# A backward kernel's gelu derivative as three two-step operations instead of five single ones

## The chip, the core and the metric

One core of a Trainium2 chip. The time is the device time of one execution in microseconds; below it is the median of three runs. The core has a matmul engine (TensorE, PE; its weight loads are listed apart as PEld), VectorE (DVE), ScalarE (ACT), GpSimd (POOL) and SyncE (SP), each with its own instruction queue worked in order, and 16 DMA engines.

## What is computed

The forward function is a small speech joint network; the kernel returns its output and the gradients of all seven inputs. Everything is bfloat16.

```python
B, T, D, K, U = 2, 16000, 256, 3, 8
def _fwd_reference(x, w1, w2, g, w_f, w_g, w_o):
    h = conv(x, w1)                    # 3 taps, padded, D -> D
    h = _gelu(h)[:, ::2, :]            # tanh form of gelu, every second row
    f = conv(h, w2)
    f = _gelu(f)[:, ::2, :]
    fe = jnp.einsum("btd,de->bte", f, w_f)
    ge = jnp.einsum("bud,de->bue", g, w_g)
    j = jnp.tanh(fe[:, :, None, :] + ge[:, None, :, :])
    return jnp.einsum("btud,dv->btuv", j, w_o)

out, vjp = jax.vjp(f, x, w1, w2, g, w_f, w_g, w_o)
return (out, *vjp(grad_out))           # grad_out: [2, 4000, 8, 256]
```

(`conv` stands for the reference's pad and loop over the three taps.) The tanh form of gelu is x times sigmoid(A (x + 0.044715 x^3)) with A = 2 sqrt(2/pi). With s the sigmoid, its derivative is s + x s (1 - s) A (1 + 3 * 0.044715 x^2).

## The kernel before

The 4,000 joint positions of each of the two batches lie on one axis of 8,016 columns, with a gap of 16 between them. It is cut into 16 chunks of 512 columns (`CW`), the last of 336. Channels lie on the partitions, in two halves (`KT`), so an activation of one chunk is a tile of 128 partitions by 2 x 512.

A chunk goes through these stages, each written as a generator that yields after a piece of work:

- `conv_units`: the first convolution, on even and odd positions (`par` 0 and 1), then a gelu on each: `HT` is the activation, `G1` the derivative.
- `conv2_units`: the second convolution and its gelu: `FT` and `G2`.
- `fe_units`, then for each of the 8 prompts `u` a `tanh` (ACT, L423).
- `joint_units`: the output matmuls (L721), the gradient of `w_o` (`gwo`, L760), and `gj`: matmuls of `grad_out` with the transposed `w_o` into PSUM (L672), which DVE evicts as `NGZ` times the tanh's derivative (L676). The square that this needs, `JSQ`, is ACT's (L664). POOL adds up the eight NGZ (L695) in `ACCN`; the last sum is `NGFE`.
- backward, of the chunk before: `d1_units` (NGFE times transposed `w_f`, evicted by DVE as `GF` with the factor `G2`, L462), `d5_units` (GF times transposed `w2`, evicted as `GH` with the factor `G1`, L486), `row_units`, `gwf_units`, `gw2_units`, `ghr_units` and `e_units` (transposes, weight gradients, the gradient of x; L496, L546, L564, L627, L640).

The main loop (L865) runs over the chunks n = 0 to 15; one pass is called a step here and takes about 49.8 us when steady. In step n, `weave` alternates the joint's units of chunk n with a fill: the convolutions of chunk n + 1 and the backward stages of chunk n - 1. The work of a gelu does not stand in these generators. `gelu` (L287) returns two lists of operations. `first` (square, sum, sigmoid, product) makes the activation and goes into the queue `later`, which `weave` pumps two at a time. `second` makes the derivative. Those of a chunk's three gelus go into the queue `late` when its second convolution is through (L381), that of the second convolution first, then `seconds0`, those of the two parities; behind them stands a one-column copy of `G1` from the chunk before, on POOL (L352). `late` is pumped one at a time and emptied at the end of the step (L904). From chunk 2 on its operations are pinned, that is, kept in program order with each other; elsewhere the compiler's scheduler may reorder instructions that don't depend on each other.

In `gelu`, `x_` is the convolution's value, `sq_` the square 0.044715 x^2, `s_` first the sum and then the sigmoid, `h_` the activation and `gp_` the derivative.

Matmul results go through a PSUM pool of 7 tiles (`psp`, L124), which are given out in turn, whatever the stage; the eighth, `GWO_ps`, is kept for the gradient of `w_o`. Scratch tiles of a gelu have three buffers each (`gel`), NGZ three (`ngzp`), JSQ two (`jsp`), the rows of the x gradient two (`gxp`).

Of the kernel before, what the change touches and what calls it, by code (L numbers as in the profile page):

```python
# [15 lines left out]
ALU = mybir.AluOpType  # L16
# [2 lines left out]
GELU_K = 0.044715  # L19
GELU_R = float(np.sqrt(0.044715))  # L20
GELU_A = float(2.0 * np.sqrt(2.0 / np.pi))

P = 128
KT = 2
# [4 lines left out]
CW = 512  # L29
# [3 lines left out]
def kernel(  # L33
# [22 lines left out]
    nc = tc.nc  # L56
# [7 lines left out]
    def geom(n):  # L64
        c0 = n * CW
        return c0, min(CW, L - c0)
# [60 lines left out]
    def ps_f32():  # L127
        return psp.tile([P, 512], FP32, name="ps", tag="ps")
# [22 lines left out]
    S = [dict() for _ in range(G)]  # L151
# [111 lines left out]
    def scratch(name, spare):  # L263
        if spare:
            return rowp.tile([P, 8, P], BF16, name="rows")[:].rearrange("p (k a) b -> p k (a b)", k=KT)
        return gel.tile([P, KT, CW], BF16, name=name)
# [17 lines left out]
    def pinned(op, n):  # L284
        return op if n <= 1 else (lambda: tc.keep_in_program_order(op()))

    def gelu(xb, W, h, gp, off, kts=((0, KT),), spare=False):  # L287

        sq, s = scratch("g_sq", spare), scratch("g_s", spare)
        TT, TS, STT = nc.vector.tensor_tensor, nc.vector.tensor_scalar, nc.vector.scalar_tensor_tensor  # L290
        first, second = [], []
        for (k0, k1) in kts:
            sq_, s_, x_ = sq[:, k0:k1, :W], s[:, k0:k1, :W], xb[:, k0:k1, :W]
            h_, gp_ = h[:, k0:k1, off:off + W], gp[:, k0:k1, off:off + W]
            first += [
                partial(nc.scalar.activation, out=sq_, in_=x_, func=ACT.Square, scale=GELU_R),
                partial(STT, out=s_, in0=sq_, scalar=1.0, in1=x_, op0=ALU.add, op1=ALU.mult),
                partial(nc.scalar.activation, out=s_, in_=s_, func=ACT.Sigmoid, scale=GELU_A),
                partial(TT, out=h_, in0=s_, in1=x_, op=ALU.mult),
            ]  # L300
            second += [
                partial(TS, out=sq_, in0=sq_, scalar1=3.0 * GELU_A, scalar2=GELU_A, op0=ALU.mult, op1=ALU.add),
                partial(TS, out=x_, in0=s_, scalar1=-1.0, scalar2=1.0, op0=ALU.mult, op1=ALU.add),
                partial(TT, out=sq_, in0=sq_, in1=x_, op=ALU.mult),
                partial(TT, out=sq_, in0=sq_, in1=h_, op=ALU.mult),
                partial(TT, out=gp_, in0=sq_, in1=s_, op=ALU.add),
            ]
        return first, second


    HALVES = ((0, 1), (1, 2))

    seconds0 = []

    def conv_units(n):
        c0, W = geom(n)
        seconds = []
        st = S[n]
        HT = htp.tile([P, 2, KT, CW + 2], BF16, name="HT")
        G1 = g1p.tile([P, 2, KT, CW + 2], BF16, name="G1")  # L320
        st["HT"], st["G1"] = HT, G1
        if n == G - 1:
            nc.gpsimd.memset(G1[:, 0, :, 2 + W:3 + W], 0.0)
        if n == 0:
            nc.gpsimd.memset(HT[:, 1, :, 1:2], 0.0)
            nc.gpsimd.memset(G1[:, 1, :, 1:2], 0.0)
        else:
            nc.gpsimd.tensor_copy(out=HT[:, 1, :, 1:2], in_=S[n - 1]["HT"][:, 1, :, CW + 1:CW + 2])
        taps = {0: ((1, 0, 0), (2, 1, 0), (0, 3, -1)), 1: ((0, 1, 0), (2, 3, 0), (1, 2, 0))}
        for par in range(2):  # L330
            xb = gel.tile([P, KT, CW], BF16, name="g_x")
            for mt in range(KT):
                ps = ps_f32()
                k = 0
                for (i, c, sh) in taps[par]:
                    for kt in range(KT):
                        nc.tensor.matmul(ps[:, :W], lhsT=W1[:, i, kt, mt * P:(mt + 1) * P],  # L337
                                         rhs=st["X", c][:, kt, 16 + sh:16 + sh + W], start=(k == 0), stop=(k == 5))
                        k += 1
                nc.scalar.copy(out=xb[:, mt, :W], in_=ps[:, :W])  # L340
                yield
            first, second = gelu(xb, W, HT[:, par], G1[:, par], 2, HALVES if n == 0 else ((0, KT),))
            if par == 1 and n > 1:
                for j in (1, 3):
                    first[j] = partial(lambda f: held.append(f()), first[j])
            later.extend(first)
            seconds += second
            if n == 0:
                pump(len(first))
        seconds0.extend(seconds)  # L350
        if n > 0:
            seconds0.append(lambda: nc.gpsimd.tensor_copy(out=G1[:, 1, :, 1:2],  # L352
                                                          in_=S[n - 1]["G1"][:, 1, :, CW + 1:CW + 2]))

    def conv2_units(n):
        c0, W = geom(n)
        st = S[n]
        HT = st["HT"]
        if n > 0:
            pump(len(later))  # L360
        FT = packed(ftp.tile([P, KT, CW], BF16, name="FT")[:], "k w", n, k=KT)
        G2 = ftp.tile([P, KT, CW], BF16, name="G2")
        st["FT"], st["G2"] = FT, G2
        xb = scratch("g_x", n == 0)
        for mt in range(KT):
            ps = ps_f32()
            k = 0
            for (i, par, off) in ((1, 0, 2), (0, 1, 1), (2, 1, 2)):
                for kt in range(KT):
                    nc.tensor.matmul(ps[:, :W], lhsT=W2[:, i, kt, mt * P:(mt + 1) * P],  # L370
                                     rhs=HT[:, par, kt, off:off + W], start=(k == 0), stop=(k == 5))
                    k += 1
            nc.scalar.copy(out=xb[:, mt, :W], in_=ps[:, :W])
            yield
        first, second = gelu(xb, W, FT, G2, 0, HALVES if n == 0 else ((0, KT),), n == 0)
        if n == 0:
            for f in first:
                f()
        else:
            later.extend(first)  # L380
        late.extend(pinned(f, n) for f in second + seconds0)  # L381
        seconds0.clear()
        late_open[0] = True
# [62 lines left out]
    def d1_units(n):  # L446
        c0, W = geom(n)
        st = S[n]
        GF = gfp.tile([P, KT, CW + 4], BF16, name="GF")
        st["GF"] = GF  # L450
        if n > 0:
            nc.gpsimd.tensor_copy(out=GF[:, :, 1:2], in_=S[n - 1]["GF"][:, :, CW + 1:CW + 2])
        else:
            nc.gpsimd.memset(GF[:, :, 1:2], 0.0)
        if n == G - 1:
            nc.gpsimd.memset(GF[:, :, 2 + W:3 + W], 0.0)
        for mt in range(KT):
            ps = ps_f32()
            for kt in range(KT):
                nc.tensor.matmul(ps[:, :W], lhsT=WFT[:, kt, mt * P:(mt + 1) * P], rhs=st["NGFE"][:, kt, :W],  # L460
                                 start=(kt == 0), stop=(kt == KT - 1))
            nc.vector.scalar_tensor_tensor(out=GF[:, mt, 2:2 + W], in0=st["G2"][:, mt, :W], scalar=-1.0,  # L462
                                           in1=ps[:, :W], op0=ALU.mult, op1=ALU.mult)
            yield

    def d5_units(n):
        st = S[n]
        c0, W = geom(n)
        N = W + 1 if n == G - 1 else W
        GF, G1 = st["GF"], st["G1"]  # L470
        GH = ghp.tile([P, 2, KT, CW + 4], BF16, name="GH")
        st["GH"] = GH
        if n == 0:
            nc.gpsimd.memset(GH[:, 0, :, 1:2], 0.0)
        else:
            nc.gpsimd.tensor_copy(out=GH[:, 0, :, 1:2], in_=S[n - 1]["GH"][:, 0, :, CW + 1:CW + 2])
        for par, taps in ((0, ((1, 0),)), (1, ((2, -1), (0, 0)))):
            for mt in range(KT):
                ps = ps_f32()
                k, last = 0, len(taps) * KT - 1  # L480
                for (i, sh) in taps:
                    for kt in range(KT):
                        nc.tensor.matmul(ps[:, :N], lhsT=W2T[:, i, kt, mt * P:(mt + 1) * P],  # L483
                                         rhs=GF[:, kt, 2 + sh:2 + sh + N], start=(k == 0), stop=(k == last))
                        k += 1
                gh = nc.vector.tensor_tensor(out=GH[:, par, mt, 2:2 + N], in0=ps[:, :N],  # L486
                                             in1=G1[:, par, mt, 2 - par:2 - par + N], op=ALU.mult)
                while held:
                    tc.add_manual_dep(held.pop().ins, gh.ins.name, NOSYNC, reason="held")
                yield  # L490
# [421 lines left out]
    n = G - 1  # L912
# [75 lines left out]
```

## Time and profile before

| | us |
|---|---|
| median of 3 runs | 823.95 |
| all three | 828.51, 820.92, 823.95 |
| the profiled execution | 822.13 |
| its span in the profile | 820.4 |

A span is the time from the first to the last instruction that the profile shows; the execution's own time has 1.7 us more around it. The profile gives for every engine its busy time, its instructions and what it waited for. A group "L277 DVE SCALAR_TENSOR_TENSOR g_s<-g_sq,g_x" is line 277 of the kernel, engine, operation, written tile and read tiles. "x29 | 60.8, 2097" is 29 instructions, 60.8 us busy, 2,097 ns mean. Two instructions of one engine can overlap by a little: the next starts when the one before is in its last stretch, so the distance from start to start is shorter than the duration. A number in brackets behind a row of the timeline is idle time of the engine ahead of it and what ended it.

Two things of the profile are used below: the TensorE clock is granted at 0.995 over the span, and the pattern of a step repeats from step 1 to step 13 to within some 10 ns in most steps (the one around 350 to 400 us holds the gap between the batches).

### The profile page before, as it was taken

How to read it: one execution, taken by the hardware profiler on the slowest of the kernel's cores; microseconds unless marked ns; L12 is line 12 of the kernel's file. 1: busy time of each engine (PE TensorE's matmuls, PEld its weight loads, DVE VectorE, ACT ScalarE, POOL GpSimd, SP SyncE). 2: the span in 40 equal slices, each digit the busy share in tenths (PEclk: the TensorE clock that was granted, in tenths of full speed). 3: DMA queues.
4: the chain of work that ended last, by engine and by line, in shares of the span. 5: the costliest groups of instructions: out<-in, count | busy, mean ns of one | idle time of the engine just before them, and what ended most of it. 6: DMA issues, size and time to landing. Idle time of an engine off the chain costs nothing.

```text
span 820.4 us, 16444 instructions
## 1 busy us (share of the span) xinstructions
PE 797.0 (97%) x6234; PEld 593.2 (72%) x6310; DVE 623.8 (76%) x1190; ACT 677.1 (83%) x1076; POOL 394.4 (48%) x419
## 2 busy tenths in 40 slices
PE   8888999999999999999999999999999999999998
PEld 3455777868678676777767778676786777778796
DVE  4995786877869778697887878868697786968634
ACT  4988997896979969799797978969799697988643
POOL 1265553553544535545476634535455345445551
PEclk9999999999999999999999999999999999999999
DMA  9989999999999999999999999999999999999944
GB/s 213 236 187 250 236 258 244 249 235 181 275 257 241 228 211 209 253 245 196 248 234 220 241 196 237 255 250 272 218 249 221 261 231 251 246 226 272 242 121 142
DMA packets 401423, 189.38 MB, mean 231 GB/s; under 512 B 349296, under 2 KB 385048, under 8 KB 401344
## 3 DMA queue, kind: packets, MB, share of 16 engines
q1 hardware_dynamic: 381104, 121.43, 80.5%
q0 software_dynamic: 20240, 66.89, 27.1%
q8 instruction: 49, 0.80, 0.5%
q14 instruction: 30, 0.25, 0.1%
HBM read 51.39 MB, written 50.34 MB: 124 GB/s over the span
## 4 chain that ended last, share of the span: by engine, by line
PE 82%; ACT 8%; DMA 4%; DVE 3%; issue 1%; SPq 1%; POOL 0%; POOLq 0%; DVEq 0%; ACTq 0%
PE GWO_ps L760 12%; PE ps L721 12%; PE ps L672 10%; PE ps L640 9%; PE ps L627 9%; PE ps L337 7%; PE ps L564 5%; PE pst L496 5%; PE ps L370 4%; PE ps L483 4%; ACT JT L423 3%; DMA JR<-JT 3%; PE ps L546 2%; PE ps L460 1%; ACT JSQ L664 1%
## 5 line engine op out<-in xcount | busy, mean ns | idle before, releaser
L695 POOL TENSOR_TENSOR ACCN<-ACCN,NGZ 128x1024 f32<-128x1024 f32 (+1 forms) x80 | 169.3, 2117 | 76.2 <-DVE NGZ L676 75.3
L676 DVE SCALAR_TENSOR_TENSOR NGZ<-JSQ,ps 128x512 bf16<-128x512 bf16 (+3 forms) x272 | 168.4, 640 | 41.0 <-PE ps L672 31.2
L723 ACT CAST OUT<-ps 128x512 bf16<-128x512 f32 (+1 forms) x252 | 145.8, 595 | 38.4 <-PE ps L721 38.3
L423 ACT ACTIVATE JT<-FE,GE 128x512 bf16<-128x512 f32 (+3 forms) x272 | 176.2, 711 | 0.5
L664 ACT ACTIVATE JSQ<-JT 128x1024 bf16<-128x1024 bf16 (+1 forms) x128 | 134.9, 1059 | 36.2 <-DVE NGZ L676 36.1
L721 PE MATMUL ps<-WO,JT 128*128 128x256 bf16 (+1 forms) x1008 | 150.6, 274 | 3.5 <-DVE NGZ L676 3.4
L760 PE MATMUL GWO_ps<-GO,JR 128*128 128x256 bf16 (+1 forms) x1008 | 149.2, 273 | 2.7 <-DMA JR<-JT 1.8
L748 POOL DMA_DIRECT2D out_dram<-OUT x76 | 55.8, 734 | 172.3 <-ACT OUT L723 156.0
L672 PE MATMUL ps<-GOT,WOT 128*128 128x512 bf16 (+1 forms) x481 | 132.6, 374 | 1.4 <-DVE W2T L845 1.0
L760 PEld LDWEIGHTS <-JR 128*128 128x128 bf16 (+1 forms) x1008 | 97.1, 98 | 29.5 <-DMA JR<-JT 3.7
L721 PEld LDWEIGHTS <-JT 128*128 128x128 bf16 (+1 forms) x1008 | 97.9, 99 | 25.8 <-issue 4.6
L627 PE MATMUL ps<-W1T,GH 128*128 128x256 bf16 (+2 forms) x756 | 100.4, 273 | 0.7
L277 DVE SCALAR_TENSOR_TENSOR g_s<-g_sq,g_x 128x1024 bf16<-128x1024 bf16 (+2 forms) x35 | 67.6, 1930 | 36.7 <-ACT g_sq L277 36.7
L627 PEld LDWEIGHTS <-GH 128*128 128x128 bf16 (+2 forms) x756 | 83.5, 116 | 13.0
L337 PE MATMUL ps<-XC,W 128*128 128x512 bf16 (+1 forms) x358 | 85.9, 377 | 1.7 <-DMA XC<-in_x_dram 1.0
L640 PE MATMUL ps<-rows,XR 128*128 128x256 bf16 (+1 forms) x708 | 84.7, 273 | 0.0
L444 DVE TENSOR_TENSOR ACC<-ACC,ps 128x512 f32<-128x512 f32 x84 | 57.5, 684 | 32.6 <-PE ps L564 26.2
L630 ACT CAST GX<-ps 128x512 bf16<-128x512 f32 (+2 forms) x126 | 72.3, 588 | 7.8 <-PE ps L627 5.2
L640 PEld LDWEIGHTS <-XR 128*128 128x128 bf16 (+1 forms) x708 | 69.3, 98 | 11.0
L259 POOL DMA_DIRECT2D out_dram<-GX x66 | 36.2, 549 | 82.8 <-ACT GX L630 81.3
L672 PEld LDWEIGHTS <-WOT 128*128 128x128 bf16 x512 | 48.2, 98 | 33.5 <-issue 2.1
L337 PEld LDWEIGHTS <-W 128*128 128x128 bf16 x384 | 37.7, 99 | 39.7 <-issue 2.1
(132 smaller groups left out, 1218.4 us busy)
## 6 DMA issues: line engine op xcount, KB each, us to landing
GO<-in_grad_out_dram SPq DMA_DIRECT2D x56, 512.0 KB, 5.7
out_dram<-OUT POOLq DMA_DIRECT2D x56, 512.0 KB, 6.0
out_dram<-GX POOLq DMA_DIRECT2D x55, 256.0 KB, 5.0
XR<-in_x_dram POOLq DMA_DIRECT2D x36, 256.0 KB, 7.8
XR<-in_x_dram POOLq DMA_DIRECT2D x12, 320.0 KB, 8.1
GO<-in_grad_out_dram SPq DMA_DIRECT2D x4, 384.0 KB, 4.9
out_dram<-OUT POOLq DMA_DIRECT2D x4, 384.0 KB, 4.4
GOT<-in_grad_out_dram SPq DMA_TRANSPOSE x68, 6.6
```

The source lines that it names most:

```text
L337: nc.tensor.matmul(ps[:, :W], lhsT=W1[:, i, kt, mt * P:(mt + 1) * P], rhs=st["X", c][:, kt, 16 + sh:16 + sh + W], start=(k == 0), stop=(k ...
L423: act = nc.scalar.activation(out=JT[:, mt, lo:hi], in_=S[n]["FE"][:, mt, lo:hi], func=ACT.Tanh, bias=GE[:, b, mt, u:u + 1], scale=1.0)
L627: nc.tensor.matmul(ps[:M, cj * D:(cj + 1) * D], lhsT=GH[:, par, kt, o:o + s * (M - 1) + 1:s], rhs=W1T[:, i, kt, :], start=(j == 0), stop=( ...
L630: nc.scalar.copy(out=t[:M, 2 * cp:2 * cp + 2, :], in_=ps[:M, :])
L640: nc.tensor.matmul(ps[:, dt * D:(dt + 1) * D], lhsT=x_row(4 * k + i + 2 * (1 - par))[:M, dt * P:(dt + 1) * P], rhs=t[:M, g + 2 * par:g + 2 ...
L664: jsq = nc.scalar.activation(out=JSQ[:, :, :W], in_=JT[:, :, :W], func=ACT.Square)
L672: nc.tensor.matmul(ps[:, :W], lhsT=WOT[:, kt, mt * P:(mt + 1) * P], rhs=GOT[:, kt, :W], start=(kt == 0), stop=(kt == KT - 1))
L676: nc.vector.scalar_tensor_tensor(out=NGZ[:, mt, lo:hi], in0=JSQ[:, mt, lo:hi], scalar=1.0, in1=ps[:, lo:hi], op0=ALU.subtract, op1=ALU.mul ...
L695: st["last"] = nc.gpsimd.tensor_tensor(out=out, in0=in0, in1=st["NGZ", u][:, :, :W], op=ALU.add)
L721: nc.tensor.matmul(ps[:M, j * V:(j + 1) * V], lhsT=st["JT", u][:, kt, o:o + M], rhs=WO[:, kt, :], start=(kt == 0), stop=(kt == KT - 1))
L723: nc.scalar.copy(out=OUT[:M, k, :], in_=ps[:M, :])
L760: nc.tensor.matmul(GWO_ps[:, dt, :], lhsT=JR[:M, j, dt, k, :], rhs=GO[:M, k, j * V:(j + 1) * V], start=(n_gwo[0] == 0), stop=(n_gwo[0] == ...
```

## The change

The list `second` of a gelu has five single operations per pair of halves: two on one tensor (`tensor_scalar`), three on two (`tensor_tensor`). For all chunks but the first it becomes three `scalar_tensor_tensor`, each of which does (in0 op0 scalar) op1 in1:

- sq = (sq + 1/3) * x
- sq = (s - 1) * sq
- gp = (sq + 1/SLOPE) * s

with SLOPE = -3 A. The result is the derivative divided by SLOPE. The factor SLOPE is put back where the derivative is used: as the scalar of GF's eviction, which has one already, and of GH's, which turns from `tensor_tensor` into `scalar_tensor_tensor`. Chunk 0 keeps the five operations and the factor 1. The copied column of G1 carries the factor of the chunk before, so POOL's copy becomes a multiplication by the ratio of the factors. The activation `h_` and the overwriting of `x_` are no longer part of the derivative.

```diff
+SLOPE = -3.0 * GELU_A
...
-    def gelu(xb, W, h, gp, off, kts=((0, KT),), spare=False):
+    def gelu(xb, W, h, gp, off, kts=((0, KT),), spare=False, scaled=True):
...
             second += [
+                partial(STT, out=sq_, in0=sq_, scalar=1.0 / 3.0, in1=x_, op0=ALU.add, op1=ALU.mult),
+                partial(STT, out=sq_, in0=s_, scalar=1.0, in1=sq_, op0=ALU.subtract, op1=ALU.mult),
+                partial(STT, out=gp_, in0=sq_, scalar=1.0 / SLOPE, in1=s_, op0=ALU.add, op1=ALU.mult),
+            ] if scaled else [
                 partial(TS, out=sq_, in0=sq_, scalar1=3.0 * GELU_A, scalar2=GELU_A, op0=ALU.mult, op1=ALU.add),
                 partial(TS, out=x_, in0=s_, scalar1=-1.0, scalar2=1.0, op0=ALU.mult, op1=ALU.add),
                 partial(TT, out=sq_, in0=sq_, in1=x_, op=ALU.mult),
                 partial(TT, out=sq_, in0=sq_, in1=h_, op=ALU.mult),
                 partial(TT, out=gp_, in0=sq_, in1=s_, op=ALU.add),
             ]
...
+    def slope(n):
+
+        return SLOPE if n else 1.0
...
-            first, second = gelu(xb, W, HT[:, par], G1[:, par], 2, HALVES if n == 0 else ((0, KT),))
+            first, second = gelu(xb, W, HT[:, par], G1[:, par], 2, HALVES if n == 0 else ((0, KT),), scaled=n > 0)
...
-            seconds0.append(lambda: nc.gpsimd.tensor_copy(out=G1[:, 1, :, 1:2],
-                                                          in_=S[n - 1]["G1"][:, 1, :, CW + 1:CW + 2]))
+            seconds0.append(lambda: nc.gpsimd.tensor_scalar(out=G1[:, 1, :, 1:2], in0=S[n - 1]["G1"][:, 1, :, CW + 1:CW + 2],
+                                                            scalar1=slope(n - 1) / slope(n), scalar2=None, op0=ALU.mult))
...
-        first, second = gelu(xb, W, FT, G2, 0, HALVES if n == 0 else ((0, KT),), n == 0)
+        first, second = gelu(xb, W, FT, G2, 0, HALVES if n == 0 else ((0, KT),), n == 0, n > 0)
...
-            nc.vector.scalar_tensor_tensor(out=GF[:, mt, 2:2 + W], in0=st["G2"][:, mt, :W], scalar=-1.0,
+            nc.vector.scalar_tensor_tensor(out=GF[:, mt, 2:2 + W], in0=st["G2"][:, mt, :W], scalar=-slope(n),
...
-                gh = nc.vector.tensor_tensor(out=GH[:, par, mt, 2:2 + N], in0=ps[:, :N],
-                                             in1=G1[:, par, mt, 2 - par:2 - par + N], op=ALU.mult)
+                gh = nc.vector.scalar_tensor_tensor(out=GH[:, par, mt, 2:2 + N], in0=G1[:, par, mt, 2 - par:2 - par + N],
+                                                    scalar=slope(n), in1=ps[:, :N], op0=ALU.mult, op1=ALU.mult)
```

## The prediction

> **What bounds the kernel now.** I read the page first, then the busy time of one 49.8 us step, then the Vector engine's groups by shape, then the engines' timelines inside that step. Parts 1 and 4 of the page:
>
> ```profile
> PE 797.0 (97%) x6234; PEld 593.2 (72%) x6310; DVE 623.8 (76%) x1190; ACT 677.1 (83%) x1076; POOL 394.4 (48%) x419
> ...
> PE 82%; ACT 8%; DMA 4%; DVE 3%; issue 1%; SPq 1%; POOL 0%; POOLq 0%; DVEq 0%; ACTq 0%
> ```
>
> The matmul engine works 97% of the span and carries 82% of the chain of waits. The busy time of one steady stretch (294.6 to 344.4 us) is tighter still; the columns are busy us of PE, weight loads, DVE, ACT, POOL, then clock and DMA:
>
> ```profile
> 294.60:344.40 49.80, 49.53 (x391) 37.09 (x394) 39.05 (x70) 42.51 (x68) 23.74 (x24) 1.00 1.12 241
> ```
>
> PE is idle 0.27 us of 49.80, and in the list of waits it waits for the Vector engine (DVE) nowhere between 140 and 690 us but for 0.2 us. So DVE has 10.75 us to spare per step and no work of its own on the path. The change touches DVE alone in size; it can gain nothing inside the steady steps, and lose only where DVE becomes so late that PE lacks something. What PE can lack is a PSUM tile: the pool has 7, given out in turn, so a tile is opened again seven openings later.
>
> **What the change puts on DVE.** Durations by shape, in the DVE groups (mean ns of one, idle before):
>
> ```profile
> L285 DVE TENSOR_SCALAR g_sq<-g_sq 128x1024 bf16<-128x1024 bf16 x39 | 16.5, 423 | 0.4
> ...
> L285 DVE TENSOR_TENSOR g_sq<-g_sq,FT 128x1024 bf16<-128x1024 bf16 x13 | 9.0, 691 | 0.4
> ```
>
> A gelu's derivative is now two one-tensor operations (0.42 each) and three two-tensor ones (0.69 each): 2.91 us when nothing disturbs. The new form is three scalar_tensor_tensor of 128x1024 bf16, both inputs in SBUF. That instruction is already in the kernel (g_s, L277). Undisturbed, early in the run:
>
> ```profile
> 31.72 1.21 DVE L277 SCALAR_TENSOR_TENSOR g_s<-g_sq,g_x 128x1024 bf16<-128x1024 bf16 x1
> 32.86 0.67 DVE L676 SCALAR_TENSOR_TENSOR NGZ<-JSQ,ps 128x512 bf16<-128x512 bf16 x1
> ```
>
> 1.21 us, the next independent instruction starting 1.14 after it; where the next one needs its result or overwrites its input it is 1.26 (another g_s starts at 53.20, its follower at 54.46). So three cost 3.63: the change adds 0.72 us per gelu, 2.2 per step, while it drops the instruction count from 15 to 9.
>
> The Trainium skill speaks for the change here: "VectorE: DVE Perf Modes", rules for kernel authors, says of chained Vector operations to keep the number of operations low, since each pays its pipeline drain. By that rule 9 for 15 would shorten DVE's work and the sum below would be zero. These rows disagree: three at 1.21 against five at 2.91.
>
> 2.2 us would vanish in the 10.75 idle if it were spread. It is not. All three derivatives of the next chunk stand together at the end of a step, between the g_s of the second convolution and the last gradient evictions NGZ (L676) of the step. I walk this place in the step at 295 us. The built program's PE order there is unchanged, instruction by instruction; DVE's is new: after g_s come first-F, ACC, FT, second-F, third-F, first-H, ACC, second-H, third-H, first-H', second-H', NGZ a, third-H', NGZ b (F: second convolution, H and H': first). Before, DVE runs so:
>
> ```profile
> 306.50 0.69 DVE L676 SCALAR_TENSOR_TENSOR NGZ<-JSQ,ps 128x512 bf16<-128x512 bf16 x1 [0.41 <-PE ps L672]
> ...
> 307.72 0.68 DVE L676 SCALAR_TENSOR_TENSOR NGZ<-JSQ,ps 128x512 bf16<-128x512 bf16 x1
> ...
> 309.87 1.17 DVE L285 TENSOR_SCALAR g_x<-g_s 128x1024 bf16<-128x1024 bf16 x1
> ...
> 312.27 2.50 DVE L285 TENSOR_TENSOR g_sq<-g_sq,HT 128x1024 bf16<-128x1024 bf16 x1
> ```
>
> NGZ a starts at 306.50, NGZ b at 307.72 and ends at 308.40. In the new order the first new instruction starts where the old one did, at 298.95. Up to NGZ b there are nine new instructions, six followed at 1.14 and three at 1.26 (10.62), two ACC at a pitch of 0.60, FT at 0.61 and NGZ a at 0.61: 13.04, so NGZ b starts at 311.99 and ends at 312.67, 4.27 late. NGZ a ends at 310.92, 3.73 late.
>
> Who waits for that: PE's weight loads show the openings of PSUM tiles (L640 is one tile of 16, L627 one of 6, L672 one of 2, L721 one of 4):
>
> ```profile
> 305.69 0.64 PEld L672 LDWEIGHTS <-WOT 128*128 128x128 bf16 x4
> 306.45 1.84 PEld L640 LDWEIGHTS <-XR 128*128 128x128 bf16 x16
> 308.30 0.21 PEld L672 LDWEIGHTS <-WOT 128*128 128x128 bf16 x2
> 308.63 0.76 PEld L627 LDWEIGHTS <-GH 128*128 128x128 bf16 x6
> 309.39 0.21 PEld L672 LDWEIGHTS <-WOT 128*128 128x128 bf16 x2
> 309.71 0.77 PEld L627 LDWEIGHTS <-GH 128*128 128x128 bf16 x6
> 310.48 0.86 PEld L721 LDWEIGHTS <-JT 128*128 128x128 bf16 x8
> ```
>
> The first row opens two tiles, those of NGZ a and b. Count seven on from b: L640, L672, L627, L672, L627, L721, L721. The second L721 tile, at 310.48 + 0.43 = 310.91, is b's buffer. It has 2.51 us to spare after 308.40; a's buffer (first L721) has 3.29 after 307.19. New: b is free at 312.67, with about 0.05 to start, so PE stands still from 310.91 to 312.72: **1.8 us per step**, the 0.5 that a costs included. PE makes it up nowhere, having 0.27 us of idle. The ACC and NGZ behind b (before at 308.66, 309.26, 310.95) become 4.0, 4.0 and 2.9 late against 2.9, 3.2 and 2.7 of room: inside the 1.8. Then DVE has caught up.
>
> The other edits, each beside this:
> - FT comes about 0.6 us later (300.69 for 300.05); its matmul starts at 302.32, and FT now ends at 301.4. Nothing; without that cover it would be as much per step.
> - GF's scalar: none. GH's eviction turns from tensor_tensor (687 ns at 128x512, L486) into scalar_tensor_tensor with one PSUM input; the same shape at L462 takes 680. Nothing.
> - POOL's column copy (0.2 us, 15 times) becomes tensor_scalar, for which there is no row: between 0.2 and the 2.1 of a full POOL addition; I take 0.2, same shape. It also moves up in POOL's queue, ahead of a GX store and the last two additions (ACCN, NGFE), and waits for third-H', done by 312.1. The additions need NGZ b and d anyway: NGFE then ends near 317.4, and its reader L460, at 318.40 before, is 1.8 later too. Even 2 us more is covered.
> - ACT: the square JSQ behind NGZ b's buffer waits to 312.7, so GX and OUT evictions run about 1.9 late, as PE does. Nothing beyond it.
> - SP: same order.
>
> **The sum.** Steps 1 to 13 hold this place with full width: 13 x 1.8 = 23.4. Step 14 prepares the last chunk, 336 columns: 0.5, scaled by width. Step 0 has the same work in another order; there five old operations stand 1.0 to 1.9 us too long behind POOL, and the new ones may meet more or fewer of these waits: 0, bounds -3 and +3. The profiled execution took 822.13 us (span 820.4 and 1.7 around it): 846.0. The runs shown (820.92, 823.95, 828.51) have their median 1.8 above it: **848 us**. With pitches off by 0.05 the stall is 1.3 to 2.3; with what the walk ignores I allow 0.8 to 3: 832 to 868.
>
> **Rivals.**
> 1. *Not slower: DVE's lateness stays inside PSUM's room.* The old TENSOR_SCALAR at 309.87 and TENSOR_TENSOR at 312.27 run 0.75 and 1.81 us longer than their undisturbed 0.42 and 0.69, just while POOL adds (308.56 to 310.75, 311.78 to 314.23). In the new order all nine are through at 311.99, and POOL's addition waits for NGZ b: 2.56 saved, more than the 2.2 added, so DVE's total is flat. But the savings lie behind NGZ b. It decides if b is under 2.51 late, that is with 1.76 / 9 = 0.2 us less per instruction (0.98 for 1.18). Then 824. Against it: g_s rows never show less than 1.2 undisturbed at this size. Chance 0.16. The skill's "SBUF — State Buffer", section on two separate sides, has an exclusive lock between GpSimd and Vector operations with two SBUF inputs; the long rows agree, ending with POOL's.
> 2. *Slower still: ACT becomes the bound.* ACT has 7.3 us idle a step, most of it late in the step, and from 305 on none. If its JSQ wait makes GX, OUT and row evictions lag more than PE does, the tightest tiles (room 0.9, near 330 us) bind next; the whole 4.3 less 0.9, 3.4 per step, gives 822 + 44 + 1.8 = 868, up to 880. Chance 0.12.
> 3. *Faster by over 1%.* All of PE's idle time is 23.4 us, most in the start and the tail; step 0 would have to get 8 shorter by fewer waits for POOL. Some 814. Chance 0.04.
>
> The forecast has 0.68. One per cent, 815.7 to 832.2, is about what this measurement tells from no change. Slower by over 1% is the forecast and rival 2: 0.80. Within: rival 1, 0.16. Range: 826 to 872 holds nearly all of the forecast, the upper third of rival 1 and half of rival 2.
>
> **What would show it.** Right: the derivative's new groups of 128x1024 at about 1210 ns; NGZ b some 13 us after the first new instruction; PE waiting for DVE NGZ L676 once per step, about 1.8 us, 25 in all; steps 51.6 us apart for 49.8. Wrong: no PE wait at L721 (rival 1), or PE waits for ACT's evictions (rival 2); new operations near 0.7 us; waits at L460 for POOL.

## The result, and the profile after

The changed kernel takes 844.65 us (median of 6 runs, 843.81 to 852.5); the kernel before 822.43 (median of 6, the three known ones among them, 819.56 to 832.03). The ratio is 1.0272, with a 95% interval from 1.0228 to 1.0316: slower by 22 us. Some runs are longer at a lower granted clock, whatever the kernel; those more than 1.5% above the fastest run of their kernel are left out of all ratios. The profiled execution took 847.4 us, its span is 845.6 at a granted clock of 0.995.

Parts 1 and 4 of the page after:

```profile
PE 800.3 (95%) x6234; PEld 592.7 (70%) x6310; DVE 621.5 (73%) x1100; ACT 678.8 (80%) x1076; POOL 397.1 (47%) x419
...
PE 66%; DVE 18%; ACT 9%; issue 4%; DMA 2%; POOL 0%; SPq 0%; DVEq 0%; ACTq 0%; POOLq 0%
```

DVE is busy 2.3 us *less* than before (621.5 for 623.8) with 90 instructions fewer, and the kernel is 22 us slower. What changed is the chain of waits: DVE's share went from 3% to 18%. The same steady stretch as before, now from 304.72 to 356.16 us (columns: busy us of PE, weight loads, DVE, ACT, POOL, then clock and DMA):

```profile
304.72:356.16 51.44, 49.82 (x391) 37.06 (x395) 38.55 (x66) 42.60 (x67) 23.87 (x24) 1.00 1.10 219
```

No engine is busy more than 0.3 us longer than before; the step is 1.6 us longer and PE idles 1.62 us of it, for 0.27 before. Whom PE waits for, in the list of PE's waits (engine, line, whom; total us, times, longest):

```profile
PE ps L730 <- DVE NGZ L685: 24.1, 29, 3.0
PE ps L346 <- DMA XC<-in_x_dram: 3.0, 1, 3.0
```

Before, the first of these was 3.4 us in 2 waits. (Lines after the new ones are 9 higher: the output matmul L721 is now L730, NGZ L685, GH L495, the derivative L286.) The place itself, in DVE's timeline of the step at 306 us; each row is start, duration, operation, and in brackets idle time ahead of it:

```profile
306.35 2.73 DVE L278 SCALAR_TENSOR_TENSOR g_s<-g_sq,g_x 128x1024 bf16<-128x1024 bf16 x1 [0.62 <-ACT g_sq L278]
309.12 1.23 DVE L286 SCALAR_TENSOR_TENSOR g_sq<-g_sq,g_x 128x1024 bf16<-128x1024 bf16 x1
...
320.38 0.68 DVE L685 SCALAR_TENSOR_TENSOR NGZ<-JSQ,ps 128x512 bf16<-128x512 bf16 x1
...
320.98 1.22 DVE L286 SCALAR_TENSOR_TENSOR G<-g_sq,g_s 128x1024 bf16<-128x1024 bf16 x1
322.12 0.68 DVE L685 SCALAR_TENSOR_TENSOR NGZ<-JSQ,ps 128x512 bf16<-128x512 bf16 x1
```

and in PE's:

```profile
320.09 0.82 PE L636 MATMUL ps<-W1T,GH 128*128 128x256 bf16 x6
321.11 0.60 PE L730 MATMUL ps<-WO,JT 128*128 128x256 bf16 x4 [0.21 <-DVE NGZ L685]
322.86 0.60 PE L730 MATMUL ps<-WO,JT 128*128 128x256 bf16 x4 [1.15 <-DVE NGZ L685]
```

From the first new instruction to NGZ b are 13.00 us, with no idle time between. Matmul ends are modelled, so I measure the two gaps from the starts of the weight loads ahead of these matmuls, less their usual distance: 0.37 and 1.31, together 1.68 us. The second matmul group starts 0.06 us after NGZ b has ended (322.12 + 0.68 = 322.80).

How far it goes for every step: I take the weight load that opens NGZ a's tile (L672, after L681) and its distance from one step to the next. Of the kernel before it is 49.77 us in the steady steps, of the changed one 51.44. This **step distance** is the best ruler of the study, since it repeats to some 0.02 us in most steps while the whole time scatters by several us. PE's weight loads come in the same order in the steady steps of all kernels of this study, so places in the step can be compared one by one.

### The profile page after: what moved, and what is told of

The parts are those of the page before. It is cut to its first block, busy times and chain, and to the rows that moved or that the text cites. A ratio compares the mean times of both kernels' runs of the same rounds, so it can differ in the third digit from the quotient of the medians.

```text
span 845.6 us, 16354 instructions
## 1 busy us (share of the span) xinstructions
PE 800.3 (95%) x6234; PEld 592.7 (70%) x6310; DVE 621.5 (73%) x1100; ACT 678.8 (80%) x1076; POOL 397.1 (47%) x419
## 4 chain that ended last, share of the span: by engine, by line
PE 66%; DVE 18%; ACT 9%; issue 4%; DMA 2%; POOL 0%; SPq 0%; DVEq 0%; ACTq 0%; POOLq 0%
PE GWO_ps L769 10%; PE ps L730 10%; PE ps L346 8%; PE ps L681 8%; PE ps L636 5%; PE ps L573 5%; PE pst L505 5%; PE ps L649 5%; DVE g_sq L286 5%; PE ps L492 4%; DVE G L286 4%; PE ps L379 3%; DVE g_s L278 3%; DVE NGZ L685 3%; ACT JT L432 2%
## 5 line engine op out<-in xcount | busy, mean ns | idle before, releaser
L685 DVE SCALAR_TENSOR_TENSOR NGZ<-JSQ,ps 128x512 bf16<-128x512 bf16 (+3 forms) x272 | 167.5, 640 | 68.1 <-PE ps L681 51.3
L673 ACT ACTIVATE JSQ<-JT 128x1024 bf16<-128x1024 bf16 (+1 forms) x128 | 134.1, 1052 | 57.2 <-DVE NGZ L685 57.2
L730 PE MATMUL ps<-WO,JT 128*128 128x256 bf16 (+1 forms) x1008 | 151.4, 272 | 24.5 <-DVE NGZ L685 24.1
L432 ACT ACTIVATE JT<-FE,GE 128x512 bf16<-128x512 f32 (+3 forms) x272 | 172.2, 703 | 0.5
L681 PE MATMUL ps<-GOT,WOT 128*128 128x512 bf16 (+1 forms) x481 | 133.7, 377 | 1.4 <-DVE W2T L854 1.0
L730 PEld LDWEIGHTS <-JT 128*128 128x128 bf16 (+1 forms) x1008 | 97.1, 98 | 50.3 <-issue 27.7
L346 PE MATMUL ps<-XC,W 128*128 128x512 bf16 (+1 forms) x358 | 86.6, 379 | 3.7 <-DMA XC<-in_x_dram 3.0
L681 PEld LDWEIGHTS <-WOT 128*128 128x128 bf16 x512 | 48.4, 98 | 33.8 <-issue 3.0
L346 PEld LDWEIGHTS <-W 128*128 128x128 bf16 x384 | 37.7, 99 | 42.1 <-issue 4.9
```

The source lines that it names most:

```text
L432: act = nc.scalar.activation(out=JT[:, mt, lo:hi], in_=S[n]["FE"][:, mt, lo:hi], func=ACT.Tanh, bias=GE[:, b, mt, u:u + 1], scale=1.0)
L673: jsq = nc.scalar.activation(out=JSQ[:, :, :W], in_=JT[:, :, :W], func=ACT.Square)
L681: nc.tensor.matmul(ps[:, :W], lhsT=WOT[:, kt, mt * P:(mt + 1) * P], rhs=GOT[:, kt, :W], start=(kt == 0), stop=(kt == KT - 1))
L685: nc.vector.scalar_tensor_tensor(out=NGZ[:, mt, lo:hi], in0=JSQ[:, mt, lo:hi], scalar=1.0, in1=ps[:, lo:hi], op0=ALU.subtract, op1=ALU.mul ...
L730: nc.tensor.matmul(ps[:M, j * V:(j + 1) * V], lhsT=st["JT", u][:, kt, o:o + M], rhs=WO[:, kt, :], start=(kt == 0), stop=(kt == KT - 1))
```

## The experiments

Two ideas were open behind the result. **A**, the prediction's: the pile of derivatives makes NGZ a and b late, and PE loses only what exceeds the room of their PSUM tiles (3.29 us for a, 2.51 for b). **B**: DVE's longer work, or the new evictions, cost by their sum, wherever they stand. Later a third came up: **the new order** alone. The built program does not only hold longer instructions; it also has a larger part of the pile ahead of NGZ a and b (8 and 9 of 9 operations, for 9 and 10 of 15 before).

The first four runs cut the change in parts.

**1. Only the evictions and POOL's column change; the derivative stays in five operations.**

```diff
-        return SLOPE if n else 1.0
+        return 1.0
...
-            first, second = gelu(xb, W, HT[:, par], G1[:, par], ..., scaled=n > 0)
+            first, second = gelu(xb, W, HT[:, par], G1[:, par], ..., scaled=False)
...
-        first, second = gelu(xb, W, FT, G2, 0, ..., n == 0, n > 0)
+        first, second = gelu(xb, W, FT, G2, 0, ..., n == 0, False)
```

> The evictions part alone: all derivatives in the five old operations, all factors 1; GH's eviction is a scalar_tensor_tensor and POOL's column copy a multiplication, as after the change. Theory A (PE loses 1.7 us per step because NGZ b, the second gradient eviction of prompt 6, is over 2.6 us late): NGZ b is on time, no PE wait at the output matmuls, as before: 820 to 826. Rival C (the changed evictions or POOL's multiplication cost the time): 840 or more.

Measured: 821.11 us, ratio 0.9971 (0.993 to 1.0013), step distance 49.77. The evictions and POOL's multiplication cost nothing here.

**2. New derivative for the second convolution's gelu alone.**

```diff
-            first, second = gelu(xb, W, HT[:, par], G1[:, par], ..., scaled=n > 0)
+            first, second = gelu(xb, W, HT[:, par], G1[:, par], ..., scaled=False)
...
-                                                            scalar1=slope(n - 1) / slope(n), scalar2=None, op0=ALU.mult))
+                                                            scalar1=1.0, scalar2=None, op0=ALU.mult))
...
-                                                    scalar=slope(n), in1=ps[:, :N], op0=ALU.mult, op1=ALU.mult)
+                                                    scalar=1.0, in1=ps[:, :N], op0=ALU.mult, op1=ALU.mult)
```

> Only the second convolution's gelu has the three-operation derivative (with GF's factor); the two gelus of the first convolution keep five. Theory A: by the built order NGZ b follows some 9.4 us after the first derivative operation for 8.8 before, 0.6 late, under its room of 2.6: no loss, 820 to 826. Rival B (each gelu's 0.72 us of added DVE work shows in the time): a third of the 22 us, about 830.

Measured: 823.36 us, ratio 1.0019 (0.997 to 1.0068), step distance 49.77. One gelu of three costs nothing.

**3. New derivative for the two gelus of the first convolution alone.**

```diff
-        first, second = gelu(xb, W, FT, G2, 0, ..., n == 0, n > 0)
+        first, second = gelu(xb, W, FT, G2, 0, ..., n == 0, False)
...
-            nc.vector.scalar_tensor_tensor(out=GF[:, mt, 2:2 + W], ..., scalar=-slope(n),
+            nc.vector.scalar_tensor_tensor(out=GF[:, mt, 2:2 + W], ..., scalar=-1.0,
```

> Only the two gelus of the first convolution have the three-operation derivative (with GH's factor). Theory A: by the built order NGZ a is 2.2 late (room 3.3), NGZ b 2.7 (room 2.6), the ACC behind it 3.5 (room 2.9): 0.6 lost per step, 13 times, 8 us: 826 to 834. Rival B: two thirds of the 22 us, about 837.

Measured: 822.81 us, ratio 0.9987 (0.9944 to 1.0029), step distance 49.92, which is 0.15 more than before. The expectation counted on ACC's lateness as well, and missed. NGZ b was 2.72 late against 2.51 of room, which makes 0.21; that alone fits, and the weight loads show a gap of 0.15 at b's tile and none elsewhere. The two parts together cost 0.15 a step, the whole change 1.67: the loss is not a sum over the gelus, it sets in past a point.

**4. The whole change, but the third gelu's pile put behind NGZ a and b.** Forty empty entries hold its last operations in the queue until the end of the step.

```diff
-        late.extend(pinned(f, n) for f in second + seconds0)
+        late.extend(pinned(f, n) for f in second + seconds0[:-4])
+        late.extend([lambda: None] * 40 * (n > 1))
+        late.extend(pinned(f, n) for f in seconds0[-4:])
```

> The changed kernel, with the last gelu's three operations put behind the last gradient evictions of the step (no-ops in the queue ahead of them); DVE's work is the same as after the change. Theory A: NGZ b is 0.7 us late, no PE wait there; the deferred three delay only evictions with 2.5 us of room: 821 to 828. Rival B (the added DVE work): 843 to 847. Rival C: 843 to 847.

Measured: 826.21 us, ratio 1.0046 (0.9995 to 1.0098), step distance 49.77, with three steps at and behind the batch seam 1 to 2 us longer than before, for which I have no cause. The same stretch of a step, in the same columns as above:

```profile
296.10:345.87 49.77, 49.77 (x396) 37.08 (x394) 40.04 (x64) 42.61 (x67) 24.08 (x24) 1.00 1.07 236
```

DVE has the same instructions as in the changed kernel, here busy even 1.5 us longer, and PE does not idle at all. Its timeline, behind NGZ b, shows where the longer time comes from:

```profile
309.34 0.68 DVE L687 SCALAR_TENSOR_TENSOR NGZ<-JSQ,ps 128x512 bf16<-128x512 bf16 x1
...
309.94 0.68 DVE L687 SCALAR_TENSOR_TENSOR NGZ<-JSQ,ps 128x512 bf16<-128x512 bf16 x1
...
314.04 3.03 DVE L286 SCALAR_TENSOR_TENSOR g_sq<-g_s,g_sq 128x1024 bf16<-128x1024 bf16 x1
```

An instruction of 1.22 us takes 3.03 while POOL adds (its NGFE runs from 313.00 to 315.99), and it costs nothing: the rescales behind it come 1.0 to 1.3 us later in the step than before, and PE waits for none of them. So B falls: it is the place of the work on DVE that costs. What this run can't say is whether the length of the instructions matters, or only the order.

**5. The old operations in a new order, first try.** The kernel before, with the pile pumped two at a time.

```diff
-            pump_late(1)
+            pump_late(2)
```

> The kernel before, the derivative queue pumped two at a time: all 15 old operations now stand ahead of NGZ a, or all but the last one, as the nine do after the change. Theory A with both parts needed (order and longer instructions): NGZ a is 2.8 us late (room 3.3), NGZ b 2.2 (room 2.6): 820 to 827. If the order alone makes the loss: 840 to 847.

Measured: 841.81 us, ratio 1.0214 (1.0119 to 1.031), step distance 50.89. This run changes part of the computation: the queue of the derivatives ran ahead of the gelu's own first operations, so some derivatives are made from values that are not final. And its loss is not where either theory has it: NGZ b is 2.45 late, and PE waits for neither NGZ at the output matmul in the steady steps; 1.1 us a step is lost in small pieces elsewhere, in most steps the largest are 0.28, 0.21 and 0.21, some 18 to 22 us behind NGZ b. It is no fair test of the order; run 8 does it again, and there the place of this loss is explained.

**6. More work in the old order.** The kernel before with one 128x1024 `tensor_tensor` more in every gelu but chunk 0's, its result used by nothing.

```diff
                 partial(TT, out=sq_, in0=sq_, in1=h_, op=ALU.mult),
+                *[partial(TT, out=x_, in0=sq_, in1=s_, op=ALU.mult)] * (1 if ... else 0),
                 partial(TT, out=gp_, in0=sq_, in1=s_, op=ALU.add),
```

> The kernel before, with one more tensor_tensor of 128x1024 in each gelu's derivative (into a tile that is not read again): 2.1 us more DVE work per step, as much as the change adds, but as built NGZ b still stands behind ten operations. Theory A: NGZ b less than 1 us late, no loss there, 820 to 828. Rival B (the added DVE work as such): about 844.

Measured: 832.0 us as the median of four runs (823.78, 825.06, 838.94 and 843.98), too scattered for a ratio; the profiled run took 825.06. Its step distance is 49.77. That is 2.1 us more DVE work a step, as much as the change adds, and NGZ a and b stand where they stood before (0.00 late both): one of the three additions runs ahead of NGZ b, and the scheduler let one old operation fall behind it, so that ten stand ahead of b as before. No loss in the steady step, against B once more.

**7. One operation more ahead of NGZ a and b in the changed kernel**, a `scalar_tensor_tensor` that overwrites x after its last use; its result is used by nothing.

```diff
+            if par == 1 and n > 1:
+                x_ = xb[:, :, :W]
+                second.insert(1, partial(nc.vector.scalar_tensor_tensor, out=x_, in0=x_, scalar=1.0, in1=x_,
+                                         op0=ALU.mult, op1=ALU.mult))
```

> The changed kernel with one more scalar_tensor_tensor of 128x1024 in the third gelu, ahead of NGZ a (into a tile that is not read again): ten ahead of NGZ b for nine. Theory A: past the room every us of lateness is lost: 1.2 more per step, 13 times, 15.6: 857 to 863. Rival B: as the 2.2 us added per step cost 22, 1.2 more cost 12: 854 to 858. Rival D (a wait of fixed length, such as ACT's for its square): 845 to 848.

Measured: 843.58 us, ratio 1.0252 (1.0185 to 1.0319), step distance 51.28. More work, and 0.16 us a step *less* than the changed kernel: a miss. PE's timeline and DVE's at the place:

```profile
318.46 1.03 PE L733 MATMUL ps<-WO,JT 128*128 128x256 bf16 x8 [1.35 <-DVE NGZ L688]
```

```profile
317.71 0.68 DVE L688 SCALAR_TENSOR_TENSOR NGZ<-JSQ,ps 128x512 bf16<-128x512 bf16 x1
...
318.32 1.22 DVE L286 SCALAR_TENSOR_TENSOR G<-g_sq,g_s 128x1024 bf16<-128x1024 bf16 x1
319.45 0.68 DVE L688 SCALAR_TENSOR_TENSOR NGZ<-JSQ,ps 128x512 bf16<-128x512 bf16 x1
```

PE waits for NGZ a, which ends at 318.39, and then runs eight matmuls, two tiles, in a row although NGZ b ends only at 320.13. So here the second L733 tile is not b's buffer. It waits for a signal of ACT, where the changed kernel's second tile waits for one of DVE. NGZ a is 4.85 late, less 3.29 of room makes 1.56; the weight loads show a gap of 1.51. Lateness against room holds; what fails is that tiles come strictly in turn. PE opens its tiles in the same order here, so I read this as the scheduler deciding which freed tile an opening takes.

**8. The old operations in the new order, second try.** Two empty entries keep the queue behind the first operations, so nothing is left out of the computation.

```diff
+        late.extend([lambda: None] * 2)
         late.extend(pinned(f, n) for f in second + seconds0)
...
-            pump_late(1)
+            pump_late(2)
```

> The kernel before, with its five short operations for the derivative, but with the pile spread so that as much of the derivative stands ahead of the step's last two rescales (NGZ a and b) as in the changed kernel: 14 of its 15 operations ahead of a and all 15 ahead of b, against 9 and 10 in the kernel before. Nothing is left out. Theory A (lateness against the room of the scratch tiles: the longer instructions AND the new place are both needed): three old derivatives take 2.2 us a step less than the new ones, so NGZ a and b end some 2 us late where a has 3.3 us of room and b 2.6; no wait at the output product behind them, steps of 49.8 us, 820 to 828 us. Theory B (the new place alone does it, the instructions' length does not matter): steps of 51.2 to 51.6, 840 to 847 us, and PE waits for NGZ at the output product once a step.

Measured: 828.83 us, ratio 1.0058 (1.001 to 1.0107), step distance 50.27. The last two rescales and the output matmuls behind them:

```profile
309.05 0.68 DVE L677 SCALAR_TENSOR_TENSOR NGZ<-JSQ,ps 128x512 bf16<-128x512 bf16 x1
...
310.26 0.68 DVE L677 SCALAR_TENSOR_TENSOR NGZ<-JSQ,ps 128x512 bf16<-128x512 bf16 x1
```

```profile
310.03 0.82 PE L628 MATMUL ps<-W1T,GH 128*128 128x256 bf16 x6
310.68 1.04 PE L722 MATMUL ps<-WO,JT 128*128 128x256 bf16 x8
```

NGZ a is 2.45 and b 2.44 late, just inside the room, and no wait stands ahead of L722. The order alone does not make the changed kernel's wait.

It is not free either: it loses 0.50 us a step, where A expected nothing. In most steps the weight loads show it in pieces of 0.07, 0.21 and 0.21, from 18 to 21 us behind NGZ b. The trace shows where the first piece of 0.21 comes from. ACT's timeline, and PE's:

```profile
311.04 1.06 ACT L665 ACTIVATE JSQ<-JT 128x1024 bf16<-128x1024 bf16 x1 [1.60 <-DVE NGZ L677]
...
330.23 0.81 ACT L499 COPY rows<-pst 128x768 bf16<-128x768 bf16 x1
```

```profile
331.09 0.60 PE L722 MATMUL ps<-WO,JT 128*128 128x256 bf16 x4
```

JSQ waits 1.60 us for NGZ b, which ends at 310.94. From there to the end of the copy at 331.04 ACT is idle for 0.07 us in all, so it makes nothing up: its copy of the rows comes 1.71 later in the step than before. The output matmul at 331.09 waits for a signal of ACT and starts 0.05 after that copy, which has freed a PSUM tile. The second piece waits for a rescale on DVE, which had itself waited 0.17 us for ACT just before. So a rescale that is in time for PE can still be too late for ACT, and PE pays some 20 us later. In run 5 the same copy is 2.35 late and the loss is 1.12: 0.64 more lateness, 0.62 more loss.

**9 and 10. The dose.** Run 8 with one, and with three, short operations more ahead of NGZ b: `HT` squared into the dead x, used by nothing.

```diff
+            x2, h2, held2 = S[n]["XB2"], S[n]["HT"][:, 1, :, 2:2 + W], seconds0[-3]
+            def padded():
+                op = held2()
+                for _ in range(1):               # 3 in run 10
+                    tc.keep_in_program_order(op)
+                    op = nc.vector.tensor_tensor(out=x2, in0=h2, in1=h2, op=ALU.mult)
+                return op
+            seconds0[-3] = padded
```

> The kernel of the run before this one (old operations, new place; step 50.27 us; NGZ a 2.45 and NGZ b 2.44 us later than in the kernel before) with one 128x1024 tensor_tensor more a step, squaring HT into the dead g_x, placed behind the third gelu's multiply with h and ahead of both NGZ a and NGZ b. Its result is used by nothing. Theory A (lateness against room, one for one beyond it): NGZ a 3.1 late inside its 3.3 of room, NGZ b 3.05 to 3.15 late against 2.51: PE waits 0.5 to 0.65 us for b once a step, steps of 50.8 to 50.9, 834 to 838 us. Rival (the place of the pile in the order sets the loss, whatever its length): 50.27 and 828 us, no wait.

Measured: 830.6 us, ratio 1.0106 (1.0031 to 1.018), step distance 50.26.

```profile
312.51 0.69 DVE L285 TENSOR_TENSOR G<-g_sq,g_s 128x1024 bf16<-128x1024 bf16 x1
313.11 0.68 DVE L687 SCALAR_TENSOR_TENSOR NGZ<-JSQ,ps 128x512 bf16<-128x512 bf16 x1
...
313.72 0.68 DVE L687 SCALAR_TENSOR_TENSOR NGZ<-JSQ,ps 128x512 bf16<-128x512 bf16 x1
```

The scheduler put the last operation, G, ahead of NGZ a too, so a is 3.66 late (room 3.29) and b 3.05 (room 2.51). The weight loads show gaps of 0.32 and 0.17 at the two tiles, 0.49 in all, where b's 0.54 was expected. The wait came as theory A has it; the step distance did not, for run 8's 0.50 elsewhere is gone: 50.26 is the 49.77 of before and this 0.49. Two waits of one step did not add up. ACT's copy of the rows is as late here as in run 8, 1.71, and ends at 333.89; but PE, held 0.49 by the first pause, opens that tile only at 334.14 and finds it free. The pause gave ACT the time that it lacked.

> The same with three such operations, one of them ahead of NGZ a and all three ahead of NGZ b. Theory A: a 3.1 late, inside its room; b 4.3 to 4.5 late against 2.51: PE waits 1.8 to 2.0 us for b once a step, as much as in the changed kernel though every derivative operation is one of the old short ones; steps of 52.1 to 52.3, 850 to 856 us. Rival: 50.27 and 828 us, no wait.

Measured: 849.32 us, ratio 1.033 (1.0271 to 1.0389), step distance 51.81. Of the three, one was built ahead of a, one between a and b, and one behind b, followed by G:

```profile
322.47 0.68 DVE L687 SCALAR_TENSOR_TENSOR NGZ<-JSQ,ps 128x512 bf16<-128x512 bf16 x1
...
323.07 0.69 DVE L389 TENSOR_TENSOR g_x<-HT 128x1024 bf16<-128x1024 bf16 x1
323.68 2.62 DVE L285 TENSOR_TENSOR G<-g_sq,g_s 128x1024 bf16<-128x1024 bf16 x1
326.22 0.67 DVE L455 TENSOR_TENSOR ACC<-ACC,ps 128x512 f32<-128x512 f32 x1
```

```profile
323.21 0.60 PE L732 MATMUL ps<-WO,JT 128*128 128x256 bf16 x4 [0.33 <-DVE NGZ L687]
...
326.95 0.60 PE L732 MATMUL ps<-WO,JT 128*128 128x256 bf16 x4 [1.08 <-DVE ACC L455]
```

a is 3.06 late, b 3.06: the gap at b's tile is 0.49, for 0.55 by the room and 1.8 to 2.0 expected. But G now stands behind b, where POOL adds (323.31 to 325.75), takes 2.62 us for 0.69, and ACC behind it comes late for the fourth tile: 1.25 more. At the third, which waits for ACT, it is 0.32. Together 2.06, and 51.81 is 2.04 above 49.77. The size expected of the wait was met through another tile than the one expected.

All runs on one ruler. Late is NGZ's start, counted from the last rescale ahead of g_s, less the same in the kernel before; excess is the larger of (a less 3.29) and (b less 2.51), or zero; the wait is the gap in the weight loads at those tiles:

| kernel | a late | b late | excess | wait there | step distance |
|---|---|---|---|---|---|
| before | 0 | 0 | 0 | 0 | 49.77 |
| 1 evictions alone | 0.00 | 0.00 | 0 | 0 | 49.77 |
| 6 more work, old order | 0.00 | 0.00 | 0 | 0 | 49.77 |
| 2 second convolution | 0.85 | 0.57 | 0 | 0 | 49.77 |
| 4 third gelu behind | 1.33 | 0.71 | 0 | 0 | 49.77 |
| 8 old operations, new order | 2.45 | 2.44 | 0 | 0 | 50.27 |
| 3 first convolution | 2.19 | 2.72 | 0.21 | 0.15 | 49.92 |
| 9 one short operation more | 3.66 | 3.05 | 0.54 | 0.49 | 50.26 |
| 10 three more | 3.06 | 3.06 | 0.55 | 0.49, and 1.57 behind it | 51.81 |
| 7 one long one more | 4.85 | 5.37 | 1.56 (a; b's tile not in use) | 1.51 | 51.28 |
| the change | 3.73 | 4.25 | 1.74 | 1.68 | 51.44 |

From no excess to 1.74 us, whichever instructions caused it, the wait is the excess less 0.05 or 0.06. What the table leaves open, the 0.50 of run 8, is ACT's by these rows. Its copy of the rows, measured in the same way, is 1.71 late in run 8 and 2.35 in run 5, and the losses are some 1.22 less, 0.50 and 1.12. In the other kernels that lateness less 1.22 is no more than what PE has already waited, and adds nothing (the changed kernel: 1.82 late, 1.68 waited).

## Why the prediction was right

**What bounds the kernel.** Right: PE has no idle time in the steady step, DVE's own time is not on the path, and the change could lose only through late PSUM tiles. After, PE idles 1.62 us in that step, and its waits for NGZ went from 3.4 to 24.1 us in all.

**The price of the new instruction.** 1.21 us each was predicted; the new groups by shape:

```profile
L286 DVE SCALAR_TENSOR_TENSOR G<-g_sq,g_s 128x1024 bf16<-128x1024 bf16 x39 | 47.7, 1223 | 0.9
L286 DVE SCALAR_TENSOR_TENSOR g_sq<-g_sq,g_x 128x1024 bf16<-128x1024 bf16 x39 | 47.6, 1220 | 0.5
L286 DVE SCALAR_TENSOR_TENSOR g_sq<-g_s,g_sq 128x1024 bf16<-128x1024 bf16 x39 | 47.5, 1219 | 0.4
```

1,219 to 1,223 ns. The rule on fewer operations, from "VectorE: DVE Perf Modes" in the Trainium skill, is answered by these rows: three of them cost 3.66 us where five cost 2.91. The work fell in count and rose in time.

**The walk through the pile.** 13.04 us from the first new instruction to NGZ b predicted, 13.00 measured; lateness 3.73 and 4.27 predicted, 3.73 and 4.25 measured. What the walk took from the built order, and did not weigh by itself, is that the lateness has two sources. Longer instructions with the third gelu behind the rescales (run 4) make b 0.71 late; the old ones in the new order (run 8) 2.44; both together 4.25. Neither alone passes the room.

**The room of the tiles.** 2.51 for b and 3.29 for a: right, and shown by the table. The sentence it rested on, that the seven tiles are "given out in turn, so a tile is opened again seven openings later", is not a rule of this kernel. It held at these two tiles. It fails at the second output tile of run 7, and in the changed kernel itself at the third, which waits for ACT where it waited for DVE before.

**The stall.** 1.8 us a step predicted, of which 0.5 from a; measured 1.68, of which 0.37. In the sum, 13 steps of 1.8 make 23.4; measured are 21.5 (most steps 1.67 more, 51.44 for 49.77, one at the seam 1.76, and one 1.28 because the kernel before has a longer step there). PE's waits for NGZ were forecast as "25 in all", which fits the sum in us; the list has 24.1 us, in 29 waits, since each step has two.

**The other steps.** Step 14: 0.5 predicted, 0.3 measured. Step 0: 0 with bounds of 3 predicted; NGZ a's opening comes 3.58 later than before in step 0 and 3.45 in step 1, but in the profiled execution the first load of x landed late: PE's start at L346 waits 2.98 us, for 1.01 before. Already the group of first-convolution matmuls that starts at 12.63 before starts at 15.38, 2.75 later, before any derivative is computed; so 0.7 to 0.8 is left for the change. The five runs beside the profiled one fit: four of them lie between 843.81 and 844.74. So the profiled execution, 847.4 for a forecast of 846.0, came near by luck: its steps were 1.9 short of the forecast, and the late load added 2.75. The median of 848 was 3.4 too high, for those 1.9 and because the 1.8 us that the median of before stood above its profiled run did not carry over (before's second median, 822.43, is 0.3 above it).

**FT, GF, GH, SP.** FT comes at 310.86, against 300.05 before; less the shift of 10.15 between the traces that is 0.66 late, and PE does not wait for it in the steady steps. GH's eviction takes 683 ns for 687, and neither run 1, which has it, nor run 2, which has GF's factor, loses anything.

**POOL's column.** 0.2 us predicted "same shape", between bounds of 0.2 and 2.1. After the change:

```profile
316.05 0.84 POOL L361 TENSOR_SCALAR G<-G 128x2 bf16<-128x2 bf16 x1
```

0.84 us, and it does not wait for third-H', as the prediction had it, but runs ahead of it. It starts inside DVE's instruction from 315.59 to 316.81 and ends 0.08 after it. In run 1 the same operation takes 0.24, starting 0.05 ahead of DVE's next. Inside the bounds, off as a value, and covered: POOL has only a store to issue between it and NGZ b, and waits 4.43 us for b.

**ACT.** The forecast had JSQ wait to 312.7, which is 322.8 in this trace; it starts at 322.90 after 1.70 us behind NGZ. ACT's waits for NGZ rose from 36.1 to 57.2 us in all, and PE's waits at L730 for ACT's JT are 0.2. Rival 2 did not come: in the steady steps PE has no gap beyond the one place. But its mechanism is there, and near the place that it named: run 8 loses its 0.50 to an ACT that is late by the wait of JSQ, with 1.22 us of room where the rival had 0.9. The changed kernel escapes it because PE waits 1.68 of ACT's 1.82 itself.

**Rival 1**, lateness inside the room, had its second half right: the old long instructions beside POOL's additions vanish. The group `g_sq<-g_sq,HT` had a mean of 1,527 ns before, and the new groups of L286 have no instruction above 1,227 (those of chunk 1, L283, still have some, up to 3.15 us). DVE's total is lower for it. But, as the text said, the saving stands behind NGZ b, where nobody waits. Its turning point of 2.51 us is what runs 8, 3 and 9 found from both sides. "SBUF — State Buffer" of the Trainium skill, section on two separate sides, has the exclusive lock that the prediction named. Runs 4 and 10 agree with it as the rows before did: 3.03 for 1.22 and 2.62 for 0.69, both while POOL adds.

No version tried is faster than the kernel before. Run 1 equals it; run 4 keeps the new derivative and loses no more than 1%.

## What to carry to other kernels

On an engine that is not the bound, count not the work that an edit adds but how late it makes the evictions behind it, and compare that with how long the matmul engine can do without their tiles: past that room each microsecond is lost once per step. Within it, look who else waits for the same evictions: an engine without idle time, as ACT here, carries the lateness on to its own tiles. Of the two losses the larger is what a step paid here. Price a fused instruction by a row of its own shape before counting instructions; three here were dearer than five. And compare the built orders: the scheduler answers longer instructions with another order and another assignment of tiles, and by run 8 that made 2.44 of the 4.25 us of lateness here.

## What was not expected of the hardware

- The engine's busy total fell by 2.3 us (621.5 for 623.8) while its work got 2.2 us longer per step by undisturbed prices, because the waits beside POOL went; and the kernel lost 22 us. In the other direction, run 4's DVE is busy 40.04 us in a step for 38.55 and loses nothing there.
- A POOL instruction on 128x2 elements takes 0.24 us when it starts ahead of a DVE instruction with two SBUF inputs (run 1) and 0.84 when it starts inside one.
- Two waits of one step need not add: run 8 loses 0.50 us a step where PE waits for ACT, run 9 has 0.49 where it waits for NGZ, with ACT as late, and both have a step distance of 50.26 to 50.27.
